# Second layer's negative slope on ScalarE, maximum and sum in one wide VectorE instruction

## The chip, the cores and the metric

The kernel runs on one core of a Trainium2 chip. The metric is the time of one execution on the device in microseconds. Engines are named as in the profile: PE is TensorE, ACT is ScalarE, DVE is VectorE, POOL is GpSimd, SP is SyncE, which issues the transfers.

## What is computed

Chunked attention (8 batches, 8 heads, 576 tokens, chunks of 64) gives 4608 tokens of width 512. Two feed-forward layers follow, each 512 to 2048 to 512. The change lies in the second, whose activation has its own negative slope for each of the 2048 hidden columns:

```python
def _moe2_ref(x, w_in, w_out, alpha):
    h = x @ w_in
    g = np.maximum(h, 0.0) + alpha * np.minimum(h, 0.0)
    return (g @ w_out).astype(np.float32)
```

`alpha` is drawn between 0 and 0.3. All data are float32.

## The kernel before

The kernel holds activations transposed: hidden columns on the 128 partitions, tokens along the row. So `alpha` of one hidden tile is one value per partition.

Attention and the first layer run together until about 920 us; then comes the second layer (`second_layer`). It multiplies 2 x 2 blocks with seven products instead of eight. Tokens go in five pairs of halves (`PAIRS`: 512, 512, 512, 384, 384 tokens per half). For each pair there are four groups (`gr`), each with four of the sixteen hidden tiles: tiles j and j+1 of the first half, and tiles j+8 and j+9 of the second. That makes 20 groups. A group has seven products i = 1 to 7 into hidden values (`h_item`), and seven products out of them (`y_item`). Each operand is split in a high part (rounded, by ScalarE) and a low part (the rest, by VectorE), and three of the four partial products are computed.

The h products accumulate in two double banks of PSUM, psHa and psHb. After each product `h_after` takes what a bank holds: after 1, 6 and 5 ScalarE copies it to g11, g12 and g22 (L698); after 2, 7 and 3 VectorE adds a bank to g11, g22 and g12 (L701), which completes them; after 4 bank a holds g21 complete. A g tile has 128 partitions and 1024 columns (two hidden tiles of 512 tokens; 768 columns for the pairs with 384).

The activation of a complete g tile is made in two steps. `relus` is two wide ScalarE instructions: `neg` = relu(-h) (L671) and, for g itself, relu(h) in place (L672); for product 4 both read the bank. Two steps of the clock later `leaks` is two half-wide VectorE instructions (L675), one per hidden tile, since `minus_alpha` differs by tile:

```python
nc.vector.scalar_tensor_tensor(
    out=g, in0=neg, scalar=minus_alpha[:, f:f + 1], in1=g, op0=ALU.mult, op1=ALU.add
)
```

There are two `neg` tiles, used in turn. Then GpSimd makes the block sums for the y products (`diff`, L725: t = g12 - g11, t2 = g22 - t, t3 = g22 - g12, t4 = g21 - t2; VectorE makes three of these in the last group). ScalarE makes the high part of each operand (`op_hi`, L715), VectorE the low part (`op_lo`, L720). The y products accumulate in psYa and psYb, and VectorE adds a bank to `yacc` (L791; ScalarE copies in the first group of a pair, L789). For the next pair of token halves the same engines make the x operands (L548, L562, L566).

The order is written out by hand. Each engine executes its queue in the order in which the program issues, and `at(when, fn)` sets the step of a clock at which a function is issued; the clock counts one for an h half product and two for a y product. `plan_group` and `plan_pair` hold the table of steps.

Of the kernel before, what the change touches and what calls it, by code (L numbers as in the profile page):

```python
# [14 lines left out]
AF = mybir.ActivationFunctionType  # L15
ALU = mybir.AluOpType
# [33 lines left out]
def tile_chunk_attention_two_ffn(  # L50
# [14 lines left out]
    nc = tc.nc  # L65
# [432 lines left out]
    NJ = NF // 2  # L498
# [3 lines left out]
    def wide(home, n):  # L502

        return home[:, :2 * n].rearrange("p (c n) -> p c n", c=2)
# [99 lines left out]
    def second_layer():  # L604
# [3 lines left out]
        minus_alpha = const.tile([P, NF], F32, name="minus_alpha")  # L608
        nc.vector.tensor_scalar(
            out=minus_alpha, in0=alpha_sb, scalar1=-1.0, scalar2=None, op0=ALU.mult  # L610
# [23 lines left out]
        clock = now = 0  # L634

        def at(when, fn, *args):
            due.setdefault(when, []).append((fn, args))
# [27 lines left out]
        def next_neg(n):  # L665
            neg_turn.append(negs[len(neg_turn) % 2])
            return wide(neg_turn[-1], n)

        def relus(g, neg, src):

            nc.scalar.activation(out=neg, in_=src, func=AF.Relu, scale=-1.0)  # L671
            nc.scalar.activation(out=g, in_=src, func=AF.Relu)  # L672

        def leak(g, neg, f):
            nc.vector.scalar_tensor_tensor(  # L675
                out=g, in0=neg, scalar=minus_alpha[:, f:f + 1], in1=g, op0=ALU.mult, op1=ALU.add
            )

        def leaks(g, neg, f):
            for jj in range(2):  # L680
                leak(g[:, jj], neg[:, jj], f + jj)

        def h_after(p, gr, i, jj):


            n, j = PAIRS[p], 2 * gr
            g = lambda nm: wide(homes["g" + nm], n)
            ps = bank["a" if i in (1, 6, 7, 4) else "b"]
            src = ps[:, :, :n]
            if jj == 0:  # L690
                return
            if i == 4:
                neg = next_neg(n)
                relus(g("21"), neg, src)
                at(clock + 2, leaks, g("21"), neg, j + NJ)
                return
            if i in (1, 6, 5):
                nc.scalar.copy(g({1: "11", 6: "12", 5: "22"}[i]), src)  # L698
            else:
                nm, f = {2: ("11", j), 7: ("22", j + NJ), 3: ("12", j)}[i]  # L700
                nc.vector.tensor_tensor(out=g(nm), in0=src, in1=g(nm), op=ALU.add)  # L701

                def rest():
                    neg = next_neg(n)
                    relus(g(nm), neg, g(nm))
                    at(now + 2, leaks, g(nm), neg, f)

                at(clock + 1, rest)

# [129 lines left out]
        while hs or ys:  # L839
# [16 lines left out]
            for _ in range(2 if hs else 0):  # L856
                p, gr, i, jj = item = hs.pop(0)
                if i == H_ORDER[0] and jj == 0:
                    plan_group(p, gr, clock)
                    if gr == 0:  # L860
                        plan_pair(p, clock)
                h_item(*item)
                clock += 1
                load_wi()
                h_after(*item)
                run_due()
# [7 lines left out]
    with tc.manual_schedule():  # L874
# [75 lines left out]
        for n in range(NBLK * NF):  # L950
            blk, f = divmod(n, NF)
# [44 lines left out]
        emit_y(NBLK * NF - 1)  # L996
        banks.close()
        second_layer()


# [28 lines left out]
```

## Time and profile before

| what | us |
|---|---|
| median of 3 runs (1655.26 to 1657.14) | 1655.92 |
| the profiled execution | 1656.75 |
| its span on the core | 1654.9 |
| TensorE busy in the span | 1599.7 (97%) |
| VectorE busy | 1249.3 (75%) |
| ScalarE busy | 782.2 (47%) |
| GpSimd busy | 496.1 (30%) |

The clock that TensorE was granted is 0.992 of full speed over the span. The chain that ended last is TensorE for 67% and VectorE for 16%. A timeline row gives the start in us from the span's beginning, the length of the row in us (a row with x2 spans both instructions), the engine, the line, the operation, and in brackets the idle time ahead of it with what ended it. An idle time under the view's threshold has no bracket.

### The profile page before, as it was taken

The numbers are of one execution on the slowest core, as the hardware profiler recorded it, in microseconds if no ns is written. First come the engines' busy times: TensorE is split into PE (matmuls) and PEld (weight loads), VectorE is DVE, ScalarE is ACT, GpSimd is POOL, SyncE is SP. The second block draws the span as 40 slices with busy tenths as digits, with TensorE's granted clock in tenths as the row PEclk, the third lists the DMA queues.
The fourth block names the chain that finished last, engine by engine and source line by source line (L and its number), as shares of the span: only waits on it lengthen the run. The fifth ranks groups of instructions, "written<-read, shape, count | busy, mean of one in ns | idle before, by whom it ended". The sixth has DMA issues, their size and how long they took to land.

```text
span 1654.9 us, 25614 instructions
## 1 busy us (share of the span) xinstructions
PE 1599.7 (97%) x9259; PEld 1334.6 (81%) x9259; DVE 1249.3 (75%) x1858; ACT 782.2 (47%) x1098; POOL 496.1 (30%) x382
## 2 busy tenths in 40 slices
PE   6888999999999999999999999999999999999997
PEld 4666888888878888887888778778877888999997
DVE  7988777777776778777643367987888789888776
ACT  5554444444444544444433454555455554545543
POOL 3575122222221322222220035233522332341320
PEclk9999999999999999999999999999999999999999
DMA  9741354544444544544230567669767966997974
GB/s 239 205 131 22 73 120 111 133 114 120 105 129 102 139 120 110 129 109 124 72 134 1 185 184 242 183 177 270 227 185 183 288 191 192 236 334 229 269 246 114
DMA packets 384045, 268.08 MB, mean 162 GB/s; under 512 B 264112, under 2 KB 321968, under 8 KB 383920
## 3 DMA queue, kind: packets, MB, share of 16 engines
q1 hardware_dynamic: 383920, 266.46, 56.8%
q8 instruction: 73, 1.20, 0.3%
q14 instruction: 52, 0.43, 0.1%
HBM read 218.11 MB, written 48.23 MB: 161 GB/s over the span
## 4 chain that ended last, share of the span: by engine, by line
PE 67%; DVE 16%; ACT 3%; issue 3%; DMA 2%; SPq 1%; POOL 1%; DVEq 0%; ACTq 0%; POOLq 0%
PE psY L477 19%; PE psH L454 19%; PE psHa L656 8%; PE psYa L773 7%; PE psYb L773 6%; PE psHb L656 6%; DVE g L675 4%; DVE yacc L791 2%; DVE o L720 2%; PE psS L341 2%; DVE at L393 1%; DVE g L701 1%; DVE xop L566 1%; DMA wi2t<-wi 1%; PE psX L410 1%
## 5 line engine op out<-in xcount | busy, mean ns | idle before, releaser
L454 PE MATMUL psH<-xs,wi 128*128 128x512 f32 x1728 | 431.2, 400 | 13.3 <-DVE g L463 7.9
L477 PE MATMUL psY<-gs,wo 128*128 128x512 f32 x1728 | 414.7, 390 | 0.1
L454 PEld LDWEIGHTS psH<-xs,wi 128*128 128x128 f32 x1728 | 324.7, 191 | 86.5 <-DVE g L463 10.3
L477 PEld LDWEIGHTS psY<-gs,wo 128*128 128x128 f32 x1728 | 324.2, 188 | 68.3 <-POOL gs L124 1.0
L121 ACT CAST gs<-g 128x512 fp32r<-128x512 f32 x144 | 89.3, 620 | 332.6 <-DVE g L463 332.6
L773 PE MATMUL psYa<-o,w 128*128 128x512 f32 (+1 forms) x960 | 217.7, 372 | 10.4 <-DVE o L720 7.0
L656 PE MATMUL psHa<-xop,wi2t 128*128 128x512 f32 (+1 forms) x960 | 211.5, 369 | 3.3 <-DVE g L701 1.9
L773 PEld LDWEIGHTS psYa<-o,w 128*128 128x128 f32 x960 | 174.4, 188 | 41.6 <-DVE o L720 14.3
L656 PEld LDWEIGHTS psHa<-xop,wi2t 128*128 128x128 f32 x960 | 175.1, 188 | 28.0 <-DVE g L701 2.7
L675 DVE SCALAR_TENSOR_TENSOR g<-neg,minus_alpha,g 128x512 f32<-128x512 f32 (+1 forms) x160 | 183.2, 1185 | 10.0 <-ACT g L672 9.7
L773 PE MATMUL psYb<-o,w 128*128 128x512 f32 (+1 forms) x720 | 159.1, 369 | 0.9 <-issue 0.6
L656 PE MATMUL psHb<-xop,wi2t 128*128 128x512 f32 (+1 forms) x720 | 158.3, 368 | 0.9 <-DVE g L701 0.9
L124 DVE TENSOR_TENSOR gs<-g,gs 128x512 fp32r<-128x512 f32 x129 | 91.6, 710 | 88.6 <-ACT gs L121 87.2
L463 DVE TENSOR_TENSOR g<-psH,g 128x512 f32<-128x512 f32 x144 | 98.1, 681 | 79.9 <-ACT g L461 78.9
L725 POOL TENSOR_TENSOR tsum<-g,g 128x1024 f32<-128x1024 f32 (+1 forms) x19 | 42.6, 2245 | 358.5 <-DVE g L675 221.3
L773 PEld LDWEIGHTS psYb<-o,w 128*128 128x128 f32 x720 | 131.2, 188 | 19.6 <-DVE o L720 1.5
L656 PEld LDWEIGHTS psHb<-xop,wi2t 128*128 128x128 f32 x720 | 131.4, 188 | 18.6 <-DVE g L701 1.2
L725 POOL TENSOR_TENSOR tsum<-g,tsum 128x1024 f32<-128x1024 f32 (+1 forms) x39 | 92.4, 2370 | 169.2 <-DVE o L720 169.2
L393 DVE STREAM_TRANSPOSE at<-e 32x128 f32<-32x128 f32 x448 | 135.5, 302 | 6.7
L461 ACT ACTIVATE g<-psH 128x512 f32<-128x512 f32 x144 | 86.2, 598 | 72.8 <-PE psH L454 72.1
L671 ACT ACTIVATE neg<-g 128x1024 f32<-128x1024 f32 (+1 forms) x60 | 58.6, 976 | 124.9 <-DVE g L701 124.9
L367 POOL TENSOR_TENSOR e<-e,d 128x512 f32<-128x512 f32 x32 | 33.5, 1047 | 241.6 <-DVE d L366 208.3
(113 smaller groups left out, 1893.3 us busy)
## 6 DMA issues: line engine op xcount, KB each, us to landing
wi2t<-wi SPq DMA_DIRECT2D x280, 256.0 KB, 3.7
w<-wo SPq DMA_DIRECT2D x140, 512.0 KB, 3.9
x<-ysb SPq DMA_DIRECT2D x36, 256.0 KB, 2.5
raw<-in_moe_w_in_dram SPq DMA_DIRECT2D x16, 512.0 KB, 5.4
raw<-in_moe_w_out_dram SPq DMA_DIRECT2D x16, 512.0 KB, 4.2
raw<-in_moe_w_in_dram SPq DMA_DIRECT2D x32, 256.0 KB, 4.1
wi<-stb SPq DMA_DIRECT2D x16, 512.0 KB, 3.2
raw<-in_moe_w_out_dram SPq DMA_DIRECT2D x32, 256.0 KB, 3.8
```

What stands on the lines that cost most here:

```text
L121: nc.scalar.copy(hi, src)
L124: eng_lo.tensor_tensor(out=lo, in0=src, in1=hi.bitcast(F32), op=ALU.subtract)
L393: nc.vector.transpose(t[o * SQ:(o + 1) * SQ, :, i * SQ:(i + 1) * SQ], blocks[i * SQ:(i + 1) * SQ, :, o // 2, o % 2, :],)
L454: nc.tensor.matmul(ps, w[:, a, c], xs[:, b, c], start=(i == 0), stop=(i == 3 * KT - 1))
L461: nc.scalar.activation(out=g, in_=ps, func=AF.Sigmoid, scale=1.702)
L463: nc.vector.tensor_tensor(out=g, in0=ps, in1=g, op=ALU.mult)
L477: nc.tensor.matmul(y_t[j][t], w[:, a, t * P:(t + 1) * P], gs[:, b], start=(f == 0 and a + b == 0), stop=(f == NF - 1 and b == 1),)
L656: nc.tensor.matmul(ps, w[:, c, a], x[b][:, c], start=(k == 0 and i in (1, 2, 5)), stop=(k == 5 and i in (2, 3, 4)), skip_group_check=True,)
L671: nc.scalar.activation(out=neg, in_=src, func=AF.Relu, scale=-1.0)
L675: nc.vector.scalar_tensor_tensor(out=g, in0=neg, scalar=minus_alpha[:, f:f + 1], in1=g, op0=ALU.mult, op1=ALU.add)
L725: eng.tensor_tensor(out=wide(homes[out], n), in0=wide(homes[x], n), in1=wide(homes[y], n), op=ALU.subtract,)
L773: nc.tensor.matmul(ps[:, d, :n], w[:, jj, d, a], x[b][:, jj], start=(k == 0 and i in (1, 5, 2)), stop=(k == 5 and i in (3, 2, 4)), skip_gr ...
```

## The change

`below` replaces `relus`: ScalarE makes `neg` = relu(-h), then multiplies it in place by minus alpha, with one half-wide copy per hidden tile that takes a scale per partition (L673). g stays h itself. `join` replaces `leaks`: one wide VectorE instruction, max(g, 0) + neg, with an immediate (L679). For product 4 ScalarE first copies the bank to g21 (L694), and `below` reads that copy.

```diff
-        def relus(g, neg, src):
+        def below(neg, src, f):
 
             nc.scalar.activation(out=neg, in_=src, func=AF.Relu, scale=-1.0)
-            nc.scalar.activation(out=g, in_=src, func=AF.Relu)
-
-        def leak(g, neg, f):
+            for jj in range(2):
+                nc.scalar.activation(
+                    out=neg[:, jj], in_=neg[:, jj], func=AF.Copy, scale=minus_alpha[:, f + jj:f + jj + 1]
+                )
+
+        def join(g, neg):
+
             nc.vector.scalar_tensor_tensor(
-                out=g, in0=neg, scalar=minus_alpha[:, f:f + 1], in1=g, op0=ALU.mult, op1=ALU.add
-            )
-
-        def leaks(g, neg, f):
-            for jj in range(2):
-                leak(g[:, jj], neg[:, jj], f + jj)
+                out=g, in0=g, scalar=0.0, in1=neg, op0=ALU.max, op1=ALU.add
+            )
...
             if i == 4:
                 neg = next_neg(n)
-                relus(g("21"), neg, src)
-                at(clock + 2, leaks, g("21"), neg, j + NJ)
+                nc.scalar.copy(g("21"), src)
+                below(neg, g("21"), j + NJ)
+                at(clock + 2, join, g("21"), neg)
                 return
...
                 def rest():
                     neg = next_neg(n)
-                    relus(g(nm), neg, g(nm))
-                    at(now + 2, leaks, g(nm), neg, f)
+                    below(neg, g(nm), f)
+                    at(now + 2, join, g(nm), neg)
```

Lines below the change are one higher than before (L698 becomes L699, L720 becomes L721, and so on).

Where VectorE stands between the completion of g12 and the low part of g11 in the first group of the second pair (place A of the text below), before and after. g2_9538 is g12, g2_9540 is g21, g2_9537 is g11.

```order
L720 TENSOR_TENSOR o2_9552<-tsum_9543,o2_9551 128x1024
L675 SCALAR_TENSOR_TENSOR g2_9538<-neg_9541,minus_alpha_9525,g2_9538 128x512 x2
L804 STREAM_TRANSPOSE x_t2_9021<-yacc_9553 128x512 x2
L791 TENSOR_TENSOR yacc_9553<-psYb_9555,yacc_9553 128x1024
L675 SCALAR_TENSOR_TENSOR g2_9540<-neg_9542,minus_alpha_9525,g2_9540 128x512 x2
L791 TENSOR_TENSOR yacc_9553<-psYa_9554,yacc_9553 128x512 x2
L720 TENSOR_TENSOR o2_9546<-g2_9537,o2_9545 128x1024
```

```order
L721 TENSOR_TENSOR o2_9552<-tsum_9543,o2_9551 128x1024
L679 SCALAR_TENSOR_TENSOR g2_9538<-g2_9538,neg_9541 128x1024
L805 STREAM_TRANSPOSE x_t2_9021<-yacc_9553 128x512 x2
L792 TENSOR_TENSOR yacc_9553<-psYb_9555,yacc_9553 128x1024
L679 SCALAR_TENSOR_TENSOR g2_9540<-g2_9540,neg_9542 128x1024
L792 TENSOR_TENSOR yacc_9553<-psYa_9554,yacc_9553 128x512 x2
L721 TENSOR_TENSOR o2_9546<-g2_9537,o2_9545 128x1024
```

Nothing moved; each pair became one wide instruction, which no longer reads `minus_alpha`.

ScalarE at the same place, from the completion of g12 to the copy of the next group's g11, before and after:

```order
L671 ACTIVATE neg_9541<-g2_9538 128x1024
L672 ACTIVATE g2_9538<-g2_9538 128x1024
L671 ACTIVATE neg_9542<-psHa_9523 128x1024
L672 ACTIVATE g2_9540<-psHa_9523 128x1024
L715 CAST o2_9545<-g2_9537 128x1024
L698 COPY g2_9537<-psHa_9523 128x1024
```

```order
L671 ACTIVATE neg_9541<-g2_9538 128x1024
L673 ACTIVATE neg_9541<-neg_9541,minus_alpha_9525 128x512 x2
L694 COPY g2_9540<-psHa_9523 128x1024
L671 ACTIVATE neg_9542<-g2_9540 128x1024
L673 ACTIVATE neg_9542<-neg_9542,minus_alpha_9525 128x512 x2
L716 CAST o2_9545<-g2_9537 128x1024
L699 COPY g2_9537<-psHa_9523 128x1024
```

The high part of g11 (the cast) now stands behind one more wide instruction and two more half-wide ones. TensorE's queue is the same in both programs.

## Rows read from the trace of the kernel before

**Rows 1.** Windows view, second layer: busy us and (instructions) of each engine.
```profile
920.00:1655.00 735.00, 713.19 (x3417) 619.20 (x3415) 584.57 (x567) 370.75 (x420) 225.41 (x93) 1.00 0.74 222
```

**Rows 2.** Groups, TensorE in the second layer: busy, mean ns | idle before, releasers.
```profile
L773 PE MATMUL psYa<-o,w 128*128 128x512 f32 (+1 forms) x960 | 217.7, 372 | 10.4 <-DVE o L720 7.0 <-issue 2.4 <-ACT neg L671 0.5
L656 PE MATMUL psHa<-xop,wi2t 128*128 128x512 f32 (+1 forms) x960 | 211.5, 369 | 3.3 <-DVE g L701 1.9 <-DMA wi2t<-wi 0.9 <-ACT g L698 0.5
L773 PE MATMUL psYb<-o,w 128*128 128x512 f32 (+1 forms) x720 | 159.1, 369 | 0.9 <-issue 0.6 <-ACT o L715 0.2
L656 PE MATMUL psHb<-xop,wi2t 128*128 128x512 f32 (+1 forms) x720 | 158.3, 368 | 0.9 <-DVE g L701 0.9
```

**Rows 3.** Timelines of 1098 to 1112 us: VectorE, GpSimd, ScalarE, TensorE.
```profile
1101.20 1.40 DVE L675 SCALAR_TENSOR_TENSOR g<-neg,minus_alpha,g 128x512 f32<-128x512 f32 x2
...
1104.85 3.69 DVE L675 SCALAR_TENSOR_TENSOR g<-neg,minus_alpha,g 128x512 f32<-128x512 f32 x2
1108.46 1.28 DVE L791 TENSOR_TENSOR yacc<-psYa,yacc 128x512 f32<-128x512 f32 x2
1109.66 1.21 DVE L720 TENSOR_TENSOR o<-g,o 128x1024 fp32r<-128x1024 f32 x1
...
1102.77 2.41 POOL L725 TENSOR_TENSOR tsum<-g,g 128x1024 f32<-128x1024 f32 x1 [18.00 <-ACT o L715]
1105.12 2.87 POOL L725 TENSOR_TENSOR t<-g,g 128x1024 f32<-128x1024 f32 x1
...
1100.82 1.02 ACT L672 ACTIVATE g<-psHa 128x1024 f32<-128x1024 f32 x1
...
1109.84 0.47 PE L773 MATMUL psYa<-o,w 128*128 128x512 f32 x1
1110.92 1.43 PE L773 MATMUL psYa<-o,w 128*128 128x512 f32 x5 [0.62 <-DVE o L720]
```

**Rows 4.** Timelines of 1040 to 1056 us: VectorE, GpSimd, TensorE.
```profile
1040.43 3.54 DVE L675 SCALAR_TENSOR_TENSOR g<-neg,minus_alpha,g 128x512 f32<-128x512 f32 x2
...
1052.87 1.21 DVE L720 TENSOR_TENSOR o<-t,o 128x1024 fp32r<-128x1024 f32 x1
...
1040.59 2.84 POOL L725 TENSOR_TENSOR tsum<-g,tsum 128x1024 f32<-128x1024 f32 x1 [3.42 <-DVE o L720]
...
1053.04 0.39 PE L773 MATMUL psYa<-o,w 128*128 128x512 f32 x1
1054.13 2.11 PE L773 MATMUL psYa<-o,w 128*128 128x512 f32 x8 [0.71 <-DVE o L720]
```

**Rows 5.** Groups by form, second layer (the last row: first layer).
```profile
L675 DVE SCALAR_TENSOR_TENSOR g<-neg,minus_alpha,g 128x512 f32<-128x512 f32 x96 | 116.5, 1254 | 9.7 <-ACT g L672 9.7
...
L720 DVE TENSOR_TENSOR o<-tsum,o 128x1024 fp32r<-128x1024 f32 x36 | 43.7, 1215 | 24.1 <-ACT o L715 24.1
...
L671 ACT ACTIVATE neg<-g 128x1024 f32<-128x1024 f32 x36 | 38.2, 1062 | 78.5 <-DVE g L701 78.5
...
L121 ACT CAST gs<-g 128x512 fp32r<-128x512 f32 x143 | 88.7, 620 | 331.8 <-DVE g L463 331.8
```

**Rows 6.** Timeline of the second layer's first group: VectorE, TensorE.
```profile
946.79 1.42 DVE L675 SCALAR_TENSOR_TENSOR g<-neg,minus_alpha,g 128x512 f32<-128x512 f32 x2 [1.46 <-ACT g L672]
...
951.56 1.41 DVE L675 SCALAR_TENSOR_TENSOR g<-neg,minus_alpha,g 128x512 f32<-128x512 f32 x2 [2.22 <-ACT g L672]
952.89 1.22 DVE L720 TENSOR_TENSOR o<-g,o 128x1024 fp32r<-128x1024 f32 x1
...
954.17 2.83 PE L773 MATMUL psYa<-o,w 128*128 128x512 f32 x11 [0.96 <-DVE o L720]
```

**Rows 7.** Timeline of 1560 to 1655 us: VectorE, TensorE.
```profile
1592.97 2.86 DVE L675 SCALAR_TENSOR_TENSOR g<-neg,minus_alpha,g 128x384 f32<-128x384 f32 x2
...
1616.70 1.14 DVE L675 SCALAR_TENSOR_TENSOR g<-neg,minus_alpha,g 128x384 f32<-128x384 f32 x2
...
1601.26 2.35 PE L656 MATMUL psHb<-xop,wi2t 128*128 128x384 f32 x12 [0.87 <-DVE g L701]
```

## The prediction

> **What bounds the kernel now.** I read the windows view first, then the groups of TensorE, then the timelines of the places where TensorE stands. In the second layer TensorE is busy for 713 of 735 us; VectorE is busy for 585, ScalarE for 371 [rows 1]. So VectorE has little room and ScalarE much. The change touches neither a matmul nor a transfer, and can give back at most TensorE's idle time there: 10.4 + 3.3 + 0.9 + 0.9 = 15.5 us [rows 2]. Most of it waits for VectorE: for a low part (L720), for a drained bank (L701), or as "issue" where a bank was being emptied (L791).
>
> By place the 15.5 us fall into four sets. **Set A**, 3.9 us: the first y product of a group, six times, 0.14 to 1.45 us; one is at 1109.84 (0.12 for the bank) and 1110.92 (0.62 for the low part) [rows 3]. **Set B**, 3.9 us: products in the middle of groups, eight times, 0.07 to 0.87 us, as the 0.71 at 1054.13 [rows 4]. **The start**, 3.7 us, of which 0.96 at 954.17 [rows 6]. **The tail**, 4.1 us after 1600 us, of which 0.87 at 1601.26 [rows 7].
>
> **Why VectorE is late there.** The mean leak instruction (L675) of 512 columns takes 1254 ns [rows 5], but two of them at 1101.20 take only 1.40 us, and two at 1104.85 take 3.69 [rows 3]. In just this time GpSimd runs two subtractions, and the second of these takes 2.87 us where the first took 2.41. Both engines lose: the first leak sits until GpSimd's first subtraction ends, GpSimd's second sits until that leak ends, and the second leak sits until 1107.99. At 1040.43 it is the same: GpSimd's 2.84 us slip in between the two halves, which take 3.54 [rows 4]. The two yacc additions at 1108.46, which read PSUM, take 1.28 us and are never stretched. So a VectorE instruction with two SBUF inputs and a GpSimd instruction take turns, whole by whole, and a pair of leaks offers GpSimd a turn in its middle. The Trainium skill's page "SBUF — State Buffer", section "Who interferes with whom", says the same: an exclusive lock for an instruction with two SBUF inputs, where issue order decides who blocks. The trace agrees; by that rule a wide instruction also holds GpSimd off for longer, which is priced under the rivals.
>
> **The change part by part.**
> 1. *VectorE: 80 pairs become 80 wide instructions.* The trace has no wide scalar_tensor_tensor with an immediate. Nearest is the two-input subtraction of 1024 columns, 1215 ns [rows 5]; two leaks in sequence take 1.40 us [rows 3]. I take 1.21 us, since both stream two SBUF inputs of 1024 columns. With 1.40 as the other bound, the free-running gain of a pair is 0.0 to 0.2 us.
> 2. *GpSimd's turn.* Place A after the change [rows 3]: the g12 leak starts at 1101.20 and ends at 1102.41; GpSimd's first subtraction runs from 1102.57 to 1104.98; the wide g21 instruction has the next turn and ends at 1106.2; GpSimd's second runs until 1108.6, under the yacc additions (1.28 us, from PSUM); the low part of g11 takes its 1.21 us and ends at 1109.8 instead of 1110.87. TensorE would ask for it after one matmul, at about 1110.1: the 0.74 us are gone. Place B [rows 4]: the wide instruction starts at 1040.43, ahead of GpSimd, and ends at 1041.65; GpSimd runs until 1044.05, beside a yacc addition from PSUM, and the subtraction behind that comes 1.0 us earlier than now. The 1.0 travels down a chain of nearly full VectorE to the low part that ends at 1054.08 and is wanted at 1053.43: it comes at 1053.1, and the 0.71 are gone. So about 1 us is gained where TensorE lacks less than 0.9 in 13 of 14 places. I count 85% of 3.9 + 3.9: **−6.6 us**.
> 3. *ScalarE, three leaks of four.* The second wide relu goes (1062 ns, as the first [rows 5]); two half-wide copies with a scale per partition come. The nearest row is a 512-column instruction at 620 ns [rows 5], two in sequence about 1.15: 0.1 us later at the leak. Bounds: 0, and +1.0 if each half costs what a wide one does. The 0.2 of the wide VectorE instruction hides it. The Trainium skill's page "ScalarE: Activation LUTs" (section "What ACT_TABLE_LOAD costs") speaks against this edit: an operand per partition is said to add about 93 ns, an estimate of 0.2 us a pair. By it the sum would be a few tenths worse; no row here shows such a ScalarE instruction.
> 4. *ScalarE, product 4.* A copy from PSUM is added (1.0 us, as the relu from PSUM at 1100.82 [rows 3]), the relu follows it, and with the two copies the leak's input comes 1.4 us later. In the middle of the layer that is covered: at place A ScalarE is done at about 1103.3 instead of 1101.84, and VectorE isn't free before 1104.65. Behind it on ScalarE's queue stands the high part of g11, with room until 1109.84. Product 4's bank is free 1 us earlier, which nobody waits for. If VectorE were not late anyway, this 1.4 us would be the next wait.
> 5. *The start.* There it is. VectorE executes in order, and the g21 leak (946.79) stands ahead of L701 for g12, of the g12 leak (951.56) and of the low part (952.89) on which TensorE stands at 954.17 [rows 6]. The first comes 1.4 us later and is 0.2 shorter, the g12 chain adds 0.1 to 0.3 and gives back 0.2: **+1.4 us** (bounds +1.0, and +3.4 with all copies at their upper bound).
> 6. *The tail.* From 1616.70 on the chain is VectorE's, GpSimd idle; three pairs lie on it, the first at 1616.70 taking 1.14 us [rows 7] where a wide one of 768 columns would take 0.19 less: −0.6 us. ScalarE's added time ends before VectorE asks. The 0.87 at 1601.26 hangs on a stretched pair at 1592.97 as in set A and goes. Together **−1.4 us**.
>
> The sum: −6.6 + 1.4 − 1.4 = −6.6 us. The profiled execution took 1656.75 us, 1.85 over its span and 0.83 over the median of the runs, 1655.92. It goes to 1650.15, and the median, which I forecast, to **1649.3**.
>
> **The rivals.** *The wait only moves.* GpSimd still needs its turns, and each may stop another VectorE instruction with two SBUF inputs (L720, L566) as long as it stopped the second leak. Then only the 0.2 us of a pair is left at each place: 0.2 at the nine large places and 0.6 for the five under 0.2, 2.4 us in A and B; 0.8 in the tail; less 1.4 at the start. That is −1.8 us, 1654.1. For it: a wide instruction holds the turn for 1.2 us, so GpSimd ends later and meets what comes next. Against it: behind most leaks stands a yacc addition from PSUM, under which GpSimd's turn passes. *ScalarE becomes the bound (slower).* The place is product 4: VectorE waits in order for the second scaled copy, and behind it stand the yacc addition that frees psYa and the low part of g11. The old pair at place A ended at 1108.54; the new instruction does so too if ScalarE is 5.5 us later than 1101.84, and in groups with less room 4.3. The delay is about four scaled copies less 0.8 us, so 1.3 us per copy decides; at 1.5 it is 5.2, 0.9 lost in 19 groups, +17 us, which with the start at +3.4 and nothing gained elsewhere is about 1676. Against it: ScalarE's 512-column row lies at 620 ns. *GpSimd too late:* it may wait 1.2 instead of 0.5 us for a turn, but its results are used some us after they are ready; I price that at nothing.
>
> **How the numbers follow.** No change means within 0.2%, 3.3 us, about what a measurement of this kernel can tell. The forecast gets 0.70, the moved wait 0.20, ScalarE as the bound 0.05, other losses of that sign 0.05. The forecast's own range: all of A, B and 1601.26 gone with the start at +1.0, −8.2 us, 1647.7; half of A and B and nothing gained per pair, −3.4 us, 1652.5. The range given reaches to 1646.0 for a start that costs nothing (−9.2 us) and to 1654.6 for the moved wait. A part of that case still ends below −3.3 us: faster 0.73, same 0.18, slower 0.09.
>
> **What would show it.** Right: leaks near 1.21 us, few above 2; VectorE's busy time in the second layer down by 30 us or more; ScalarE's up by some 30 (20 copies of 1.0 and 80 times 0.1); TensorE's idle time before psYa down from 10.4 to about 4, with the wait near 954 grown by 1.4. Wrong: scaled copies over 1 us; VectorE waiting for ScalarE ahead of the g21 leak in the middle groups; L720 or L566 stretched as L675 was.

## The result and the profile after

The changed kernel takes 1641.20 us (median of 3 runs, 1641.08 to 1641.76) against 1655.92: a ratio of 0.9911, 95% interval 0.9888 to 0.9933. That is 14.7 us less where 6.6 were forecast, and below the range given. The direction was right; the size forecast was less than half of it.

The windows view of the second layer after the change, columns as in [rows 1], and the groups of TensorE, as in [rows 2]:

```profile
920.00:1640.00 720.00, 705.08 (x3416) 618.86 (x3414) 535.01 (x486) 413.77 (x520) 234.70 (x93) 1.00 0.76 226
```

```profile
L774 PE MATMUL psYa<-o,w 128*128 128x512 f32 (+1 forms) x960 | 212.1, 368 | 4.2 <-DVE o L721 1.9 <-issue 1.8 <-ACT o L716 0.4
L656 PE MATMUL psHa<-xop,wi2t 128*128 128x512 f32 (+1 forms) x960 | 211.6, 369 | 2.9 <-DVE g L702 1.7 <-DMA wi2t<-wi 0.7 <-ACT g L699 0.5
L774 PE MATMUL psYb<-o,w 128*128 128x512 f32 (+1 forms) x720 | 158.4, 368 | 0.7 <-ACT o L716 0.7
L656 PE MATMUL psHb<-xop,wi2t 128*128 128x512 f32 (+1 forms) x720 | 158.3, 368 | 0.5 <-DVE g L702 0.5
```

VectorE is busy 50 us less, ScalarE 43 us more. TensorE's idle time fell from 15.5 to 8.3 us, by 7.2, and the kernel gained twice that. Most of the other half is already in these rows: the same 960 matmuls into psYa were "busy" for 217.7 us before and for 212.1 now. So part of what TensorE lost was written down as busy time.

The groups by form, answering to [rows 5]:

```profile
L679 DVE SCALAR_TENSOR_TENSOR g<-g,neg 128x1024 f32<-128x1024 f32 x48 | 72.5, 1511 | 16.0 <-ACT neg L673 16.0
L721 DVE TENSOR_TENSOR o<-g,o 128x1024 fp32r<-128x1024 f32 x36 | 63.6, 1767 | 1.2 <-ACT o L716 1.2
L721 DVE TENSOR_TENSOR o<-tsum,o 128x1024 fp32r<-128x1024 f32 x36 | 43.8, 1216 | 27.3 <-ACT o L716 27.0
```

```profile
L673 ACT ACTIVATE neg<-neg,minus_alpha 128x512 f32<-128x512 f32 x96 | 64.2, 717 | 1.6
L671 ACT ACTIVATE neg<-g 128x1024 f32<-128x1024 f32 x48 | 51.0, 1062 | 82.3 <-DVE g L702 81.9
```

and the line of the wide instruction, shortest, median and longest in ns:

```profile
L679 DVE SCALAR_TENSOR_TENSOR g<-g,neg x80: 945/1217/3447, 934.6 to 1612.3; 128x1024 f32<-128x1024 f32 x48, 128x768 f32<-128x768 f32 x32
```

The wide instruction's median is 1217 ns; 12 of 80 are stretched by over 15%. The low part of g (L721) is now stretched instead: 1767 ns in the mean, against 1432 before the change, where the median was 1217:

```profile
L720 DVE TENSOR_TENSOR o<-g,o 128x1024 fp32r<-128x1024 f32 x36 | 51.6, 1432 | 3.0 <-ACT o L715 2.8
```

That is one of the signs that the prediction gave for being wrong, and yet the kernel gained; the account below comes back to it under the rivals.

Place A after the change, timelines of VectorE, GpSimd and TensorE, answering to [rows 3]:

```profile
1102.27 1.33 DVE L679 SCALAR_TENSOR_TENSOR g<-g,neg 128x1024 f32<-128x1024 f32 x1
1103.52 1.27 DVE L792 TENSOR_TENSOR yacc<-psYa,yacc 128x512 f32<-128x512 f32 x2
1104.71 2.22 DVE L721 TENSOR_TENSOR o<-g,o 128x1024 fp32r<-128x1024 f32 x1
```

```profile
1100.10 2.41 POOL L726 TENSOR_TENSOR tsum<-g,g 128x1024 f32<-128x1024 f32 x1 [16.26 <-DVE g L679]
1102.46 3.39 POOL L726 TENSOR_TENSOR t<-g,g 128x1024 f32<-128x1024 f32 x1
```

```profile
1105.80 2.91 PE L656 MATMUL psHb<-xop,wi2t 128*128 128x512 f32 x12
1108.55 2.88 PE L774 MATMUL psYa<-o,w 128*128 128x512 f32 x12
```

It goes as step 2 worked it out: the wide instruction has its turn whole, GpSimd waits for it (3.39 us instead of 2.41), the yacc additions run beside GpSimd, and the low part waits for GpSimd's end. It is done at 1106.93, and the y product at 1108.55 runs through without a wait.

Place B after the change, timelines of VectorE, GpSimd and TensorE, answering to [rows 4]:

```profile
1041.28 1.21 DVE L679 SCALAR_TENSOR_TENSOR g<-g,neg 128x1024 f32<-128x1024 f32 x1
...
1043.55 2.29 DVE L566 TENSOR_TENSOR xop<-x_b,xop 128x1024 fp32r<-128x1024 f32 x1
...
1052.64 1.22 DVE L721 TENSOR_TENSOR o<-t,o 128x1024 fp32r<-128x1024 f32 x1
```

```profile
1041.44 3.32 POOL L726 TENSOR_TENSOR tsum<-g,tsum 128x1024 f32<-128x1024 f32 x1 [3.43 <-DVE o L721]
```

```profile
1054.02 2.88 PE L774 MATMUL psYa<-o,w 128*128 128x512 f32 x12
```

Here too the wide instruction runs whole and GpSimd waits for it. The x subtraction (L566) then sits until GpSimd ends at 1044.76, and still the low part is done at 1053.86, ahead of the y product at 1054.02, which no longer waits.

### The profile page after: what moved, and what is told of

It is laid out like the page before. It is cut to its first block, busy times and chain, and to the rows that moved or that the text cites. A ratio compares the mean times of both kernels' runs of the same rounds, so it can differ in the third digit from the quotient of the medians.

```text
span 1639.4 us, 25619 instructions
## 1 busy us (share of the span) xinstructions
PE 1592.9 (97%) x9257; PEld 1336.1 (81%) x9259; DVE 1200.3 (73%) x1778; ACT 825.6 (50%) x1198; POOL 504.8 (31%) x382
## 4 chain that ended last, share of the span: by engine, by line
PE 81%; DVE 6%; ACT 2%; issue 1%; DMA 1%; SPq 0%; POOL 0%; DVEq 0%; POOLq 0%; ACTq 0%
PE psY L477 19%; PE psH L454 19%; PE psYa L774 12%; PE psHa L656 11%; PE psYb L774 9%; PE psHb L656 8%; PE psS L341 2%; DVE at L393 2%; PE psX L410 1%; DMA wi2t<-wi 1%; DVE g L463 1%; DVE ysb L488 0%; SPq L300 0%; DVE u L161 0%; DVE u L166 0%
## 5 line engine op out<-in xcount | busy, mean ns | idle before, releaser
L774 PE MATMUL psYa<-o,w 128*128 128x512 f32 (+1 forms) x960 | 212.1, 368 | 4.2 <-DVE o L721 1.9
L726 POOL TENSOR_TENSOR tsum<-g,tsum 128x1024 f32<-128x1024 f32 (+1 forms) x39 | 99.8, 2559 | 162.3 <-DVE o L721 162.3
L671 ACT ACTIVATE neg<-g 128x1024 f32<-128x1024 f32 (+1 forms) x80 | 78.1, 976 | 127.7 <-DVE g L702 127.1
L679 DVE SCALAR_TENSOR_TENSOR g<-g,neg 128x1024 f32<-128x1024 f32 (+1 forms) x80 | 106.2, 1328 | 19.5 <-ACT neg L673 19.5
```

What stands on the lines that cost most here:

```text
L679: nc.vector.scalar_tensor_tensor(out=g, in0=g, scalar=0.0, in1=neg, op0=ALU.max, op1=ALU.add)
L726: eng.tensor_tensor(out=wide(homes[out], n), in0=wide(homes[x], n), in1=wide(homes[y], n), op=ALU.subtract,)
L774: nc.tensor.matmul(ps[:, d, :n], w[:, jj, d, a], x[b][:, jj], start=(k == 0 and i in (1, 5, 2)), stop=(k == 5 and i in (3, 2, 4)), skip_gr ...
```

## The experiments

The kernels of each section were measured beside the kernel before, which took 1655.40, 1655.76 and 1656.20 us in the three.

### GpSimd's turn, VectorE's plain time, or something else

Three kernels change one thing each, and a fourth is the third on the changed kernel. *Halves*, from the changed kernel:

```diff
-            nc.vector.scalar_tensor_tensor(
-                out=g, in0=g, scalar=0.0, in1=neg, op0=ALU.max, op1=ALU.add
-            )
+            for jj in range(2):
+                nc.vector.scalar_tensor_tensor(
+                    out=g[:, jj], in0=g[:, jj], scalar=0.0, in1=neg[:, jj], op0=ALU.max, op1=ALU.add
+                )
```

> The change, with the wide VectorE instruction cut in two half-wide ones with an immediate; ScalarE does all that it does in the change. Theory T1 (the gain is GpSimd's turn in the middle of a pair): most of the 14.7 us are lost again, 1651 to 1657 us, leaks of 2 to 3 us are back, over 60 late starts of TensorE. Rival T2 (the gain is VectorE's plain time, 0.2 us a pair): two halves without the scalar operand take about 1.28 us, between 1.40 and 1.21, so some 60% of the gain stay: about 1647 us. Rival T3 (the gain is g freed of the relu in place and product 4's bank handed back earlier): all of it stays, 1641 us.

Measured: 1661.33 us, ratio 1.0037 (1.0022 to 1.0051) to the kernel before, so the whole gain is lost and 6 us more; that is 4 us over the range that T1 gave, and far from T2 and T3. Place A in this kernel, VectorE and GpSimd:

```profile
1105.03 1.28 DVE L680 SCALAR_TENSOR_TENSOR g<-g,neg 128x512 f32<-128x512 f32 x2
...
1108.56 3.60 DVE L680 SCALAR_TENSOR_TENSOR g<-g,neg 128x512 f32<-128x512 f32 x2
...
1113.29 1.21 DVE L722 TENSOR_TENSOR o<-g,o 128x1024 fp32r<-128x1024 f32 x1
```

```profile
1106.39 2.41 POOL L727 TENSOR_TENSOR tsum<-g,g 128x1024 f32<-128x1024 f32 x1 [17.95 <-DVE g L680]
1108.76 2.86 POOL L727 TENSOR_TENSOR t<-g,g 128x1024 f32<-128x1024 f32 x1
```

A pair that is left alone takes 1.28 us, as expected, hardly more than a wide instruction. The pair that meets GpSimd takes 3.60, nearly as before the change (3.69).

What T1 had not counted is in part in the first group. There the low part of g11 is stretched by GpSimd, and TensorE waits for it:

```profile
950.96 3.33 DVE L722 TENSOR_TENSOR o<-g,o 128x1024 fp32r<-128x1024 f32 x1 [0.24 <-ACT o L717]
```

```profile
954.35 2.93 PE L775 MATMUL psYa<-o,w 128*128 128x512 f32 x6 [2.86 <-DVE o L722]
```

The granted clock was near half for some us there as well. Counted from start to start of the matmuls (explained below), TensorE lost 9.4 us up to 980 us, against 5.0 in the kernel before. The middle of the layer lost 21.0 us against 17.0; what these 4 us come from is not shown. The late starts were some 43, not over 60 as T1 said.

*One slope*, from the kernel before, leaves out the slope per column:

```diff
-            for jj in range(2):
-                leak(g[:, jj], neg[:, jj], f + jj)
+            nc.vector.scalar_tensor_tensor(
+                out=g, in0=neg, scalar=-0.15, in1=g, op0=ALU.mult, op1=ALU.add
+            )
```

> The kernel before, with ScalarE's two relus as they were, and one wide VectorE instruction neg * (-0.15) + g in place of the two: it leaves out the slope per hidden column (one slope for all). T1: the whole gain of the change without ScalarE's added work, so 1639 to 1641 us, with the start as in the kernel before (one late start near 954 us, not three from 950 to 955). T2: the same time, since VectorE's plain time falls equally; this run tells T3 apart, by which nothing would be gained: 1655 us.

Measured: 1638.95 us, ratio 0.9903 (0.9888 to 0.9919). The wide instruction alone brings the gain, and ScalarE's added work isn't needed for it; it only makes room for a slope per column. T3 falls; T2 gives the same time as T1 here, so this kernel can't tell them apart.

*No sums*, the kernel before and the changed one, leaves out the block sums (GpSimd's, and VectorE's three of the last group); the y products that used them read tiles of ones:

```diff
+        nc.vector.memset(homes["t"], 1.0)
+        nc.vector.memset(homes["t3"], 1.0)
+
         def diff(n, out, x, y, eng):
-            eng.tensor_tensor(
-                out=wide(homes[out], n), in0=wide(homes[x], n), in1=wide(homes[y], n),
-                op=ALU.subtract,
-            )
+            pass
```

> The kernel before without the block sums of the hidden values (GpSimd's 77 subtractions and VectorE's three in the last group): the y products 5, 6, 7 and 4 read tiles of ones, so that part of the computation is left out. GpSimd then has only the x sums in the second layer. T1: without GpSimd's turns the pairs are not stretched, TensorE's late starts go, 1632 to 1643 us. T2: VectorE has as many instructions of its own as before, the time falls by less than 4 us, 1652 or more.

> The changed kernel without the same block sums. T1: with GpSimd out of the way the change is worth little: this is within 2.5 us of the kernel before without the sums (the start 1 us worse, the tail 0.5 better). T2: it is faster than that one by 10 us or more, as with the sums.

Measured: 1640.26 us from the kernel before, 1640.75 from the changed one (ratios 0.9910, 0.9893 to 0.9927, and 0.9911, 0.9895 to 0.9927). Without GpSimd's sums the change is worth nothing, and the kernel before alone falls by 15 us. Its leaks, by form:

```profile
L675 DVE SCALAR_TENSOR_TENSOR g<-neg,minus_alpha,g 128x512 f32<-128x512 f32 x96 | 67.6, 746 | 10.6 <-ACT g L672 10.6
```

746 ns in the mean where [rows 5] have 1254, and none of the 96 over 753: their stretch was GpSimd, all of it. This edit also spares the other engines the wait for GpSimd's results, but that was small: in the second layer of the kernel before three waits were for a block sum, 7.6 us together, and none of them was TensorE's. So it is GpSimd's turns that cost. T1's account fits all four. Its range of times holds without the sums, is missed by 0.05 us with *one slope* and by 4 us with *halves*. T2 fails in three.

### The start, and ScalarE's way to the leak

*Fused*, from the changed kernel; it needs slopes that aren't negative, as they are here:

```diff
-            nc.scalar.activation(out=neg, in_=src, func=AF.Relu, scale=-1.0)
             for jj in range(2):
                 nc.scalar.activation(
-                    out=neg[:, jj], in_=neg[:, jj], func=AF.Copy, scale=minus_alpha[:, f + jj:f + jj + 1]
+                    out=neg[:, jj], in_=src[:, jj], func=AF.Relu, scale=minus_alpha[:, f + jj:f + jj + 1]
                 )
...
-                out=g, in0=g, scalar=0.0, in1=neg, op0=ALU.max, op1=ALU.add
+                out=g, in0=g, scalar=0.0, in1=neg, op0=ALU.max, op1=ALU.subtract
```

> The change with its two ScalarE steps made one: each half-wide relu takes the scale minus alpha itself (relu(-alpha h) is alpha relu(-h) as long as alpha isn't negative, as it is here), and the wide VectorE instruction subtracts it. ScalarE has 80 wide instructions less. T1: GpSimd's turns are as in the change, so the middle of the layer stays; the start loses its 1.4 us and more, since the way to the leak gets 0.9 us shorter than in the kernel before: 1637.5 to 1640 us. If ScalarE's way to the leak is what still holds the middle of the layer in the change (T4): below 1636 us.

*First group old*, from the changed kernel (its `relus` and `leaks` are those of the kernel before):

```diff
...
+                if (p, gr) == FIRST_G:
+                    relus(g("21"), neg, src)
+                    at(clock + 2, leaks, g("21"), neg, j + NJ)
+                    return
                 nc.scalar.copy(g("21"), src)
...
+                    if (p, gr) == FIRST_G:
+                        relus(g(nm), neg, g(nm))
+                        at(now + 2, leaks, g(nm), neg, f)
+                        return
                     below(neg, g(nm), f)
```

> The change in all groups but the first, which keeps the two relus and the two half-wide leaks of the kernel before. The step on the start says that ScalarE's longer way costs 1.4 us there: this should be 1.0 to 2.0 us faster than the change, 1639.2 to 1640.2 us. If the start costs nothing: the same as the change within 0.5 us.

> The changed kernel itself, beside the other three on the same chip: 1641.2 us within 1 us. By T1 and the count of late starts its profile has about 16 of them in the second layer, against 41 of the kernel before.

*Fused, from the bank*, from the fused kernel; product 4's instruction reads PSUM, and is issued one step earlier:

```diff
-        def join(g, neg):
+        def join(g, neg, h=None):
...
-                out=g, in0=g, scalar=0.0, in1=neg, op0=ALU.max, op1=ALU.subtract
+                out=g, in0=g if h is None else h, scalar=0.0, in1=neg, op0=ALU.max, op1=ALU.subtract
...
-                nc.scalar.copy(g("21"), src)
-                below(neg, g("21"), j + NJ)
-                at(clock + 2, join, g("21"), neg)
+                below(neg, src, j + NJ)
+                at(clock + 1, join, g("21"), neg, src)
```

> The fused kernel, and for product 4 the wide VectorE instruction reads the bank of PSUM directly, so ScalarE's copy of it goes. That instruction then has one input in SBUF only and should never be stretched by GpSimd (T1: at most 1.3 us each). The bank is held until it has run, just when the next group's first h product wants it. T1 with the start shorter by another 1 us: 1636 to 1638.5 us. If the bank is held too long: late starts of psHa at each group, 1640 to 1650 us.

| kernel | us, median | ratio to the kernel before |
|---|---|---|
| the change again | 1642.37 | 0.9920 (0.9906 to 0.9935) |
| first group old | 1642.02 | 0.9921 (0.9906 to 0.9935) |
| fused | 1638.73 | 0.9900 (0.9887 to 0.9914) |
| fused, from the bank | 1637.77 | 0.9895 (0.9881 to 0.9908) |

The change again lies 1.2 us over its first measurement, a little outside the 1 us expected, and 18 late starts stand in its profile by the count that its expectation uses. The start in the changed kernel, TensorE and VectorE, answering to [rows 6]:

```profile
950.30 3.02 PE L656 MATMUL psHb<-xop,wi2t 128*128 128x512 f32 x12 [0.49 <-DVE g L702]
953.71 0.50 PE L774 MATMUL psYa<-o,w 128*128 128x512 f32 x1 [0.38 <-ACT o L716]
955.16 2.79 PE L774 MATMUL psYa<-o,w 128*128 128x512 f32 x11 [0.95 <-DVE o L721]
```

```profile
947.89 1.23 DVE L679 SCALAR_TENSOR_TENSOR g<-g,neg 128x1024 f32<-128x1024 f32 x1 [2.92 <-ACT neg L673]
949.04 1.22 DVE L702 TENSOR_TENSOR g<-psHb,g 128x1024 f32<-128x1024 f32 x1
952.75 1.22 DVE L679 SCALAR_TENSOR_TENSOR g<-g,neg 128x1024 f32<-128x1024 f32 x1 [2.49 <-ACT neg L673]
```

One wait became three. Two come by the chain that step 5 names: the g21 instruction waits 2.92 us for ScalarE and holds L702 back, and the low part comes late in the end. The one between is for the high part (ACT o L716), behind the same copies on ScalarE. With the first group as before, one wait of 0.97 us is left in its place:

```profile
951.74 0.39 PE L794 MATMUL psYa<-o,w 128*128 128x512 f32 x1
953.10 2.79 PE L794 MATMUL psYa<-o,w 128*128 128x512 f32 x11 [0.97 <-DVE o L741]
```

The stretch from the first second-layer matmul through the first twelve products is 1.2 to 1.3 us shorter so than in the two profiles of the change, as the step said. But the whole run was only 0.35 us faster than the change where 1.0 to 2.0 were expected. That expectation is missed. The difference lies within what repeated runs differ by, so in the time the price of the start is not shown. The fused kernel takes 3.6 us less than the change: 2.0 at the start, the rest spread; the middle of the layer lost 3.9 us by late TensorE starts in it, and 3.8 and 4.9 in the two profiles of the change. So T4 falls. ScalarE's longer way holds nothing up in the middle, though VectorE waits 19.5 us for it in all, 7.2 of them in the middle; the prediction had named such waits as a sign of being wrong.

Reading the bank has the lowest median, 1.0 us under the fused kernel, but the times of the two overlap. Its instruction, by form:

```profile
L678 DVE SCALAR_TENSOR_TENSOR g<-psHa,neg 128x1024 f32<-128x1024 f32 x12 | 14.6, 1215 | 1.8 <-ACT neg L672 1.8
```

No one of its 20 takes over 1225 ns, though 18 of them run beside a GpSimd subtraction: with one input in SBUF it was not stretched here. The bank is held too long in a few groups only (three waits of psHa, 0.8 us in all).

### What a late start costs

The change gained twice what it took away of TensorE's idle time. A count of late starts in the timelines explains the rest, and a dose of them tests the count. From the changed kernel, with 3 and with 5:

```diff
-            nc.vector.tensor_tensor(
-                out=lo, in0=wide(homes[nm], n), in1=hi.bitcast(F32), op=ALU.subtract
-            )
+            for _ in range(3 if i == 1 else 1):
+                nc.vector.tensor_tensor(
+                    out=lo, in0=wide(homes[nm], n), in1=hi.bitcast(F32), op=ALU.subtract
+                )
```

> The change, with the low part of product 1 of each group computed three times over (the same result), so VectorE has 40 more subtractions of 1.2 or 0.95 us, all ahead of one y product per group: a dose of late starts for the size. Theory S1 (a late start of TensorE costs its idle time in the profile and about 0.27 us more, since a record ends 0.16 us after the next one could have started and the second matmul behind a wait is 0.11 us slow as well): the second layer grows by the added idle time plus 0.27 us for each added late start, within 15%. S2 (the idle time is the cost, as the prediction had it): it grows by the added idle time alone. Some 10 to 25 late starts more than in the change, 1645 to 1655 us.

> The same with the low part of product 1 computed five times over: 80 more subtractions. S1: growth of the second layer over the change = added idle time + 0.27 us for each added late start, within 15%; S2: the added idle time alone. About 30 to 60 added late starts and 1665 to 1690 us, so that the two differ by 8 us or more.

Measured: 1694.19 us (ratio 1.0229, 1.0214 to 1.0244) and 1753.91 us (1.0592, 1.0574 to 1.0609), well above the ranges expected; the late starts were fewer and longer. What TensorE lost is counted from one matmul's start to the next's. In pace these are 0.227 us apart at 512 columns and 0.173 at 384. A late start is one that comes over 0.03 us after that; the second matmul behind a wait, late as well, counts with the first. Place B before the change, from TensorE's timeline, shows the cost of one:

```profile
1050.32 2.88 PE L656 MATMUL psHb<-xop,wi2t 128*128 128x512 f32 x12
1053.04 0.39 PE L773 MATMUL psYa<-o,w 128*128 128x512 f32 x1
1054.13 2.79 PE L773 MATMUL psYa<-o,w 128*128 128x512 f32 x11 [0.71 <-DVE o L720]
1056.76 2.91 PE L656 MATMUL psHa<-xop,wi2t 128*128 128x512 f32 x12
```

The twelve matmuls from 1050.32 take 2.72 us to the next start, the twelve from 1053.04 take 3.72. So 1.00 us was lost where the idle time says 0.71: a record lasts 0.39 us though the next one may start after 0.23, which hides 0.16, and the second matmul behind the wait comes 0.11 late.

Second layer (first matmul to the last one's start) against the changed kernel's 706.0 us, all in us:

| kernel | longer by | idle | late starts, x 0.27 | at the low clock | sum of the three |
|---|---|---|---|---|---|
| before | 14.9 | 7.1 | 25: 6.8 | 1.5 | 15.4 |
| halves | 21.4 | 12.0 | 26: 7.0 | 2.6 | 21.6 |
| low part 3 times | 52.5 | 35.9 | 18: 4.9 | 11.1 | 51.9 |
| low part 5 times | 111.6 | 77.7 | 15: 4.1 | 30.0 | 111.8 |

S2 falls in all four. S1 as it was written falls in the two doses, short by a fifth and a quarter; it lacked the clock. With the clock taken off, late starts are a small part of what the doses added, so the doses test the clock more than the 0.27. The 0.27 has better support elsewhere: what idle time and clock leave over, divided by the late starts, is 0.25, 0.26, 0.31 and 0.26 us in the four rows, and the 28 waits in the kernel before that show over 0.06 us of idle time cost 0.27 us beyond it in the mean, as do the 12 in the change. Why the second matmul behind a wait is late, no run here shows. The windows of the last kernel around one of its waits (the eighth column is the granted clock):

```profile
1126.00:1139.00 13.00, 9.40 (x42) 7.43 (x40) 12.86 (x13) 3.28 (x4) 5.76 (x2) 1.00 0.56 163
1139.00:1143.00 4.00, 3.87 (x10) 3.05 (x11) 4.00 (x7) 1.96 (x2) 0.34 (x1) 0.57 0.45 100
1143.00:1156.00 13.00, 13.00 (x59) 10.71 (x58) 6.41 (x4) 9.38 (x11) 5.38 (x2) 1.00 1.00 249
```

TensorE did nothing for 3.6 of 13 us, then the granted clock was near half, 1.2 instead of 2.4 GHz, for some 3.4 us. The kernel before has this once, at 1637 us behind its wait of 1.80 us:

```profile
1634.00:1637.00 3.00, 1.20 (x8) 0.91 (x7) 3.00 (x5) 0.10 (x1) 0.00 (x0) 1.00 0.00 0
1637.00:1640.00 3.00, 3.00 (x14) 2.87 (x14) 0.52 (x2) 0.00 (x0) 0.00 (x0) 0.65 0.00 0
```

and the change's first profile hasn't, though it has the same wait (1.77 us); its second profile has it again. So this 1.5 us of the 14.9 is not surely the change's.

## Why the prediction was wrong

*The step that failed* is step 2, which priced sets A and B at 85% of their idle time. It rests on the first part's sentence that the change "can give back at most TensorE's idle time there", 15.5 us. That bound was not passed as a number (the layer got 14.9 us shorter while idle time fell by 7.1), but idle time is not what a wait costs. As idle time the step was right to 0.1 us, with some luck in the 85%, which was an allowance: in the middle of the layer it fell from 7.7 to 1.1 us, by 6.7 where 6.6 were counted. But each of the waits costs some 0.27 us more than its idle time, and 11 late starts in the middle of the kernel before show less than 0.06 us of idle time or none and were not in the sets at all. From start to start the middle lost 17.0 us before and 3.8 after: **−13.2 us where the step had −6.6**. Of the difference of 6.6, the 26 late starts that went account for 7.0, by the same 0.27 each.

*The mechanism* held: turns by whole instructions, at places A and B as worked out, and [rows 3] and [rows 4] against their counterparts above show it. The Trainium skill's page "SBUF — State Buffer", section "Who interferes with whom", has this lock. The runs agree in what they could try: instructions with two inputs in SBUF are stretched, up to 3447 ns for one that takes 1217 alone, and the 20 with one input in SBUF are not (1225 ns at most).

*The start*: +1.3 us where +1.4 were counted, through the chain named. So close an agreement is in part chance: ScalarE's way to the g21 instruction grew by 1.5 us, and a wait ahead of it was 0.16 shorter in this execution.

*The tail*: −3.0 us from start to start where −1.4 were counted. The wait at 1601.26 is gone as said, and was worth 1.1 us with what stands beyond its idle time; 1.5 of the rest is the clock, which the prediction had at nothing.

*ScalarE*: the scaled copy of 512 columns takes 717 ns, not about 620; the pair 1.34 us, not 1.15. The Trainium skill's page "ScalarE: Activation LUTs", section "What ACT_TABLE_LOAD costs", was right here with its 93 ns for an operand per partition: 717 is 97 over [rows 5]'s 620. In the middle of the layer, which is covered, this cost nothing; the start is counted above.

*The rivals*: "the wait only moves" has a true half. I summed what each instruction took over its unstretched length: leaks 79 us before and 17 after, the low parts 10 and 31, the x subtractions 5 and 9. So some 61 us went from the leaks and 25 came back elsewhere. They came back where TensorE hardly waits: the middle lost 3.8 us in all. "ScalarE becomes the bound" was not reached.

## What to carry to other kernels

Where two engines take turns by whole instructions, as VectorE and GpSimd did here, cutting a stretch of work in two gives the other engine a turn in its middle; one wide instruction, or an input moved to PSUM, took it away in these runs. What a stall costs TensorE is read from start to start, against the pace of the products around it; its idle time in the profile was only a part here, and many short stalls showed no idle time at all. Of an engine that is "97% busy", look for the products whose spacing differs before taking the rest as what can be won.

## What the runs showed of the hardware

A pair of half-wide VectorE instructions that met two GpSimd instructions at place A took 3.6 to 3.7 us instead of 1.3 to 1.4, with an operand per partition (3.69) as with an immediate (3.60). Wide instructions with one input in PSUM ran beside GpSimd 18 times, none of them for more than 1225 ns. A late start of TensorE cost 0.27 us beyond its idle time (0.16 and 0.11). In or just behind some waits the granted clock fell to the lower level, 1.2 GHz: for 3.4 us behind the wait of 1.80 us in the kernel before, and not behind the same wait (1.77 us) in the change's first profile. In the dose of 5 it fell at 15 of the 20 longest waits (2.0 to 10.0 us), and not at one of 3.36 us. In the two doses this cost 11 and 30 us, a fifth to a quarter of the time added.
